# Strassen products for every other pair of feature blocks, plain products for the rest

## The chip, the cores and the metric

The kernel runs on one core of one Trainium2 chip. The metric is the device time of one execution in microseconds (us). Before the change three timed runs took 3019.33, 3019.34 and 3024.54 us (median 3019.34). Below, PE is TensorE's matmuls and PEld its weight loads, DVE is VectorE, ACT is ScalarE, POOL is GpSimd and SP is SyncE, which issues most DMAs.

## The reference

Two stages follow each other. The first transforms 8 sequences of 3008 tokens by 256 channels with a real FFT along the tokens, mixes the channels with a complex 256x256 matrix, adds a bias, shrinks the values and transforms back. The second is a two-layer network on the 24064 rows that result:

```python
X = np.fft.rfft(x, axis=1)
Yr = Xr @ w_r - Xi @ w_i + b_r ;  Yi = Xr @ w_i + Xi @ w_r + b_i
Yr, Yi = shrink(Yr, 0.01), shrink(Yi, 0.01)
y = np.fft.irfft(Yr + 1j * Yi, n=3008, axis=1)      # rows of 256
h = y @ w_in                                        # 256 -> 2048
g = np.maximum(h, 0.0) ** 2
out = g @ w_out                                     # 2048 -> 256
```

The change lies in the last line, `g @ w_out`.

## The kernel before

**Tiles and steps.** The 24064 rows are cut into 48 tiles (`tiles`, six for each of the 8 sequences) of 500 or 504 columns: the kernel holds everything transposed, features in the partitions, tokens along the columns. The 2048 features are 16 blocks of 128. A `Step(t, n)` takes tile t and the pair of feature blocks 2n and 2n+1, so a tile has 8 steps (n = 0 to 7) and the kernel 384. Each number is carried as a sum of two shorter ones, hi and lo, and every product is three matmuls: hi by hi, lo by hi, hi by lo. `win`, `wout` and the tiles `yt`, `mb`, `mt` are such couples.

**What a step does.** `block(j)` multiplies the tile by `w_in` for block j of the pair: 6 matmuls of 500 columns into a bank `psh` (there are two). ACT takes relu out of the bank (`mc<-psh`); for j = 0 DVE squares it (`mc<-psh,mc`), for j = 1 ACT squares it (`mc<-mc`). `mc` then holds four quarters: two feature blocks by two halves of the tokens. Those are the four entries of a 2x2 block matrix, and the 256 rows of `w_out` that belong to the pair, by its 256 output columns, are the other. `out(j)` multiplies the two by Strassen's scheme in Winograd's form: 7 products of 128x128 by 128x250 in place of 8. Three of them take quarters of `mc` as they are (`raw`), four take the sums T1 to T4 that POOL makes of them (`ms`, three instructions). The weights' sums S1 to S4 are made once, at the start. `split` makes hi and lo of the raw quarters (`mb`, an ACT cast and a DVE subtraction), `split_sums` of the sums (`mt`, likewise). `out(0)` is the 9 matmuls on `mb`, `out(1)` the 12 on `mt`, all of 250 columns; they add up over the tile's 8 steps in four banks (`pso0` to `pso3`).

**The tile's end.** The four banks then hold products that still have to be added to one another. `drain` copies the banks to `me` (DVE: banks 0 and 3, ACT: banks 1 and 2) and `finish` adds them on POOL, six instructions, and stores two tiles of output.

**What sets the order.** In the main loop at the end, half-step m does, for n = m // 2 and k = m % 2: `steps[n-2].out(k)`, `steps[n].block(k)`, and for k = 1 `steps[n-1].split_sums()` and `steps[n].split()`. The helper `then` chains these instructions on each engine in just this order, so each engine's queue takes them one after the other. The transforms (`Fwd`, `Pair`, `Back`; banks `psf`) of the sequences that come next are put between them by a scheduling pass: in the first seven of the eight sequences the queues hold transform work as well, in the last one nearly none. Ahead of the main loop a front part transforms the first sequence in full precision and prepares the weights from 64-bit numbers; `moe_part`, `wout_join` and `wout_sums` belong to it.

Of the kernel before, what the change touches and what calls it, by code (L numbers as in the profile page):

```python
# [10 lines left out]
F32R = mybir.dt.float32r  # L11
# [25 lines left out]
    "kv": 3, "psf": 6,  # L37
}
MAIN = {
    "xs": 1, "xe": 1, "kv": 1, "kp": 1, "kq": 1, "ksh": 1, "ksl": 1, "kxl": 1, "kb": 1, "kcm": 1, "me": 1,  # L40
}


# [6 lines left out]

A11, A12, A22, S1, S2, S3, S4 = range(7)
B11, B22, B21 = range(3)
T1, T3, T2, T4 = range(4)


# [1 line left out]
def fnet_moe(ctx: ExitStack, tc, x, w_r, w_i, b_r, b_i, w_in, w_out, bm, cm, dx, a32, c32, out):  # L59
# [14 lines left out]
    wout = [const.tile([128, NF // 2, 7, 128], F32R, name=f"wout{j}") for j in range(2)]  # L74


    front = ExitStack()
# [91 lines left out]
    def moe_part(q):  # L169
        if q < 8:  # L170
            f, c = divmod(q, 2)
            fs = slice(f * 512, (f + 1) * 512)
            return Double(
                win[0][:, c, fs], win[1][:, c, fs], w_in[c * 128:(c + 1) * 128, f * 1024:(f + 1) * 1024],
                lambda t: t.rearrange("p f t -> p (f t)"),
            )
        f = (q - 8) * 2
        return Double(
            None, None, w_out[f * 128:(f + 2) * 128, :].rearrange("(f p) d -> p f d", p=128),
            lambda t: t.rearrange("p (f d) t -> p f (d t)", f=2),  # L180
        )

# [6 lines left out]
    def wout_sums(n, pair):  # L189
        w = pair[0].wide  # L190
        a = w.rearrange("p n (f i d) -> p n f i d", f=2, i=2)
        a11, a21, a12, a22 = (a[:, :, f, i] for f in range(2) for i in range(2))
        st = T("ds", [128, 2, 4, 128], F32)
        s1, s2, s3, s4 = (st[:, :, j] for j in range(4))
        dve.tensor_add(out=s1, in0=a21, in1=a22)
        sub(dve, s2, s1, a11)
        sub(dve, s3, a21, a11)
        sub(dve, s4, a12, s2)
        hi, lo = (v[:, n:n + 2] for v in wout)
# [262 lines left out]
    def then(eng, op, *args, **kwargs):  # L462
        with tc.issue_after(last_of[eng].ins) if eng in last_of else nullcontext():
            last_of[eng] = op(*args, **kwargs)  # L464

    def then_halves(hi, lo, v):
        then(act, copy, act, hi, v)
        then(dve, sub, dve, lo, v, hi)

    class Step:  # L470
# [3 lines left out]
        def block(self, j):  # L474
# [14 lines left out]
            if j == 0:  # L489
# [4 lines left out]
            self.raw, self.sum = (  # L494
                [T(f"m{v}{k}", [128, n * HM], F32R)[:, :n * h].rearrange("p (j h) -> p j h", j=n) for k in range(2)]
                for v, n in (("b", 3), ("t", 4))
            )
# [9 lines left out]
        def split_sums(self):  # L507
            then_halves(self.sum[0], self.sum[1], self.s)

        def out(self, j):  # L510
            t, n, h = self.t, self.n, self.h
            if n == j == 0:
                acc[t] = [bank([128, 2, 256], f"pso{d}")[:, :, :h] for d in range(4)]
            o = acc[t]

            products = (
                ((S4, self.raw, B22, o[0], 0), (A12, self.raw, B21, o[0], 1), (A11, self.raw, B11, o[1], 0)),
                ((S2, self.sum, T2, o[1], 1), (S1, self.sum, T1, o[2], 0), (S3, self.sum, T3, o[2], 1),
                 (A22, self.sum, T4, o[3], 0)),
            )[j]  # L520
            for a, g, b, ps, i in products:
                for k, (w, v) in enumerate(((0, 0), (1, 0), (0, 1))):
                    then(
                        pe, pe.matmul, ps[:, i], wout[w][:, n, a], g[v][:, b], start=n == k == i == 0,
                        stop=n == NF // 2 - 1 and k == 2 and (i == 1 or a == A22),
                    )
            if n == NF // 2 - 1:
                self.drain(j)

        def drain(self, j):  # L530
            t, h = self.t, self.h
            o = acc[t]
            if j == 0:
                e = T("me", [128, 8 * HM], F32)[:, :8 * h].rearrange("p (j h) -> p j h", j=8)
                acc[t].append(e)
                copy(dve, e[:, 0:2], o[0])
                return
            e = o[4]
            copy(act, e[:, 6:8], o[1])
            copy(act, e[:, 4:6], o[2])  # L540
            copy(dve, e[:, 3], o[3][:, 0])


        def finish(self, k):
            t, h = self.t, self.h
            e = acc[t][4]
            c22, c21, p5, p7, p1, u2 = (e[:, j] for j in range(2, 8))
            if k == 6:
# [7 lines left out]
            add = (  # L556
                (u2, u2, p1), (c22, p5, p7), (e[:, 4:6], e[:, 4:6], u2.unsqueeze(1).broadcast_to([128, 2, h])),
                (e[:, 0:2], e[:, 0:2], e[:, 4:8:2]), (c22, c22, u2), (c21, c21, p7),
            )[k]
            pool.tensor_tensor(out=add[0], in0=add[1], in1=add[2], op=ALU.add)  # L560


    def pair_tasks(pairs, start, step):
# [34 lines left out]

    ring = [Fwd32(0, q, 2) for q in range((J + 1) // 2)]
    units = [Unit32(0, g) for g in range(G)]  # L600
    parts = [moe_part(q) for q in (0, 1, 8, 9, 2, 3, 10, 11, 4, 5, 12, 13, 6, 7, 14, 15)]

    for f in ring[:FRONT["big"]]:
        f.load()
# [7 lines left out]
    extra = []  # L612
    for n, p in enumerate(parts):
        k = n * 13 // 10
        if n % 4 == 2:
            extra += [(k + 3, lambda n=n: wout_join(parts[n:n + 2]))]
        extra += [(k - 1, p.load), (k + 3, lambda p=p, u=units[k]: p.bits(u)), (k + 3, p.join)]
        if n % 4 < 2:
            extra += [(k + 3, p.split)]
        elif n % 4 == 3:  # L620
            extra += [(k + 3, lambda n=n: wout_sums(n // 4 * 2, parts[n - 1:n + 1]))]
    extra.sort(key=lambda j: j[0])
    last = units[2]
    for r in range(-5, len(units) + 3):
# [28 lines left out]
    for m in range(2 * len(steps) + 11):  # L653
# [25 lines left out]
        if ends:  # L679
            ends.pop(0)()  # L680
        if k and n % (NF // 2) == 1 and n > 1:
            ends += [lambda u=steps[n - 2], j=j: u.finish(j) for j in range(7)]
        while jobs and jobs[0][0] < r + 1:
            jobs.pop(0)[1]()

# [85 lines left out]
```

## Time and profile before

| | |
|---|---|
| median of 3 runs | 3019.34 us |
| the profiled execution: its time, its span | 3021.53 us, 3019.6 us |
| PE busy | 2707.3 us (90%), 16856 matmuls |
| POOL, DVE, ACT busy | 2277.0 (75%), 1984.2 (66%), 1757.7 us (58%) |
| mean granted TensorE clock | 0.976 |
| DMA | 250.41 MB, 83 GB/s on the mean |
| first matmul of the main loop (`psh`) | 156 us from the start |

The span runs from the first to the last instruction, and the busy time of PE is the union of its matmuls' records, whose ends are modelled: a matmul's record is longer than the time until the next may start. So PE's time is read below from the starts of matmuls that follow each other, and from its waits.

### The profile page before, as it was taken

Reading aid. Unit: us, or ns where it says so; the run is one execution under the profiler, and the core shown is the slowest. Engines: PE = TensorE matmul, PEld = TensorE weight load, DVE = VectorE, ACT = ScalarE, POOL = GpSimd, SP = SyncE. Lnnn points to the kernel's source line nnn. Section 1 sums busy time; section 2 is a strip of 40 time slices with the busy share of each in tenths; the row PEclk is TensorE's granted clock in tenths of the full one; section 3 lists DMA queues with packets and bytes.
Section 4 is the critical chain, followed back from the end, with each engine's and each line's share of the span. In section 5 each row is a group of like instructions: output and inputs, shape, how many; then the busy total and the mean of one; then the engine's idle time right before and its main releaser. Section 6 shows DMA issues by size and latency. Waiting matters only on the chain.

```text
span 3019.6 us, 46324 instructions
## 1 busy us (share of the span) xinstructions
PE 2707.3 (90%) x16856; PEld 2392.2 (79%) x16856; DVE 1984.2 (66%) x2651; ACT 1757.7 (58%) x3178; POOL 2277.0 (75%) x2082
## 2 busy tenths in 40 slices
PE   5699988899999999999999998999999999988887
PEld 4588877788878888888878888888887888877776
DVE  5846676577657766577656777567765777755554
ACT  3465655565556655656556565566656666555554
POOL 3387768687788867878788777888778886777776
PEclk8899999899999999999999999999999999999999
DMA  8432233322242223322323222322224222210000
GB/s 242 156 104 89 65 94 90 99 79 86 66 115 73 84 79 89 100 77 77 91 85 94 75 84 80 99 80 79 84 64 123 73 75 74 74 40 23 30 8 14
DMA packets 191253, 250.41 MB, mean 83 GB/s; under 512 B 21755, under 2 KB 135667, under 8 KB 191027
## 3 DMA queue, kind: packets, MB, share of 16 engines
q1 hardware_dynamic: 178627, 224.85, 24.5%
q0 software_dynamic: 12400, 22.61, 3.4%
q8 instruction: 134, 2.20, 0.3%
q14 instruction: 92, 0.75, 0.1%
HBM read 146.85 MB, written 100.53 MB: 82 GB/s over the span
## 4 chain that ended last, share of the span: by engine, by line
PE 36%; DVE 19%; POOL 18%; ACT 14%; issue 6%; DMA 2%; SPq 0%; POOLq 0%; DVEq 0%; ACTq 0%
PE pso L464 15%; PE psh L464 15%; DVE mt L94 10%; POOL ms L94 7%; ACT mt L90 6%; ACT mc L464 5%; POOL me L560 5%; POOL xs L233 4%; PE psf L301 4%; DVE kv L322 3%; DVE mb L94 2%; DMA du<-s 1%; POOL yt L94 1%; PE psf L236 1%; DVE mc L464 1%
## 5 line engine op out<-in xcount | busy, mean ns | idle before, releaser
L464 PE MATMUL psh<-yt,win 128*128 128x500 f32 (+1 forms) x4608 | 1211.6, 396 | 1.4 <-DVE mc L464 1.2
L94 DVE TENSOR_TENSOR mt<-ms,mt 128x1000 fp32r<-128x1000 f32 (+1 forms) x384 | 579.1, 1508 | 711.1 <-ACT mt L90 710.3
L464 PEld LDWEIGHTS psh<-yt,win 128*128 128x128 f32 x4608 | 825.3, 191 | 125.1 <-DVE mc L464 2.0
L94 POOL TENSOR_TENSOR ms<-mc,ms 128x250 f32<-128x250 f32 (+1 forms) x768 | 875.7, 1140 | 46.5
L464 PE MATMUL pso<-mt,wout 128*128 128x250 f32 (+1 forms) x4608 | 711.6, 293 | 193.6 <-DVE mt L94 167.5
L464 ACT ACTIVATE mc<-psh 128x500 f32<-128x500 f32 (+1 forms) x768 | 451.9, 588 | 697.3 <-PE psh L464 694.7
L464 PEld LDWEIGHTS pso<-mt,wout 128*128 128x128 f32 x4608 | 607.3, 192 | 282.8 <-DVE mt L94 223.4
L94 POOL TENSOR_TENSOR ms<-mc 128x500 f32<-128x500 f32 (+1 forms) x384 | 503.8, 1312 | 330.4 <-ACT mc L464 318.1
L94 DVE TENSOR_TENSOR mb<-mc,mb 128x750 fp32r<-128x750 f32 (+1 forms) x384 | 540.6, 1408 | 3.2 <-ACT mb L90 2.5
L464 PE MATMUL pso<-mb,wout 128*128 128x250 f32 (+1 forms) x3456 | 501.6, 283 | 1.7 <-DVE mb L94 1.7
L464 PEld LDWEIGHTS pso<-mb,wout 128*128 128x128 f32 x3456 | 473.8, 190 | 34.1 <-DVE mb L94 1.9
L90 ACT CAST mt<-ms 128x1000 fp32r<-128x1000 f32 (+1 forms) x384 | 391.6, 1020 | 62.6 <-POOL ms L94 62.3
L90 ACT CAST mb<-mc 128x750 fp32r<-128x750 f32 (+1 forms) x384 | 314.4, 819 | 0.0
L560 POOL TENSOR_TENSOR me<-me 128x250 f32<-128x250 f32 (+3 forms) x288 | 295.3, 1048 | 15.3 <-ACT me L90 12.5
L464 DVE SCALAR_TENSOR_TENSOR mc<-psh,mc 128x500 f32<-128x500 f32 (+1 forms) x384 | 256.5, 668 | 12.7 <-ACT mc L464 11.1
L464 ACT ACTIVATE mc<-mc 128x500 f32<-128x500 f32 (+1 forms) x384 | 239.8, 625 | 9.2
L94 POOL TENSOR_TENSOR yt<-dy,yt 128x376 fp32r<-128x376 f32 (+3 forms) x168 | 149.9, 894 | 114.6 <-ACT yt L90 113.7
L233 POOL TENSOR_TENSOR xs<-xt 120x256 f32<-120x256 f32 x182 | 187.1, 1048 | 35.4 <-PE psf L236 34.5
L301 PE MATMUL psf<-wx,kxh 128*128 128x256 f32 x1008 | 203.6, 282 | 4.6 <-DVE kul L94 4.6
L90 ACT CAST yt<-dy 128x376 fp32r<-128x376 f32 (+3 forms) x168 | 71.8, 432 | 192.9 <-DVE dy L446 119.9
L322 DVE TENSOR_TENSOR kv<-psf,ke 64x256 f32<-64x256 f32 x336 | 141.2, 420 | 46.2 <-PE psf L301 41.9
L301 PEld LDWEIGHTS psf<-wx,kxh 128*128 128x128 f32 x1008 | 165.0, 189 | 8.0 <-DVE kul L94 6.0
(89 smaller groups left out, 2680.3 us busy)
## 6 DMA issues: line engine op xcount, KB each, us to landing
du<-s SPq DMA_DIRECT2D x128, 256.0 KB, 3.1
s<-kuh SPq DMA_DIRECT2D x192, 128.0 KB, 2.1
s<-kul SPq DMA_DIRECT2D x192, 128.0 KB, 2.1
s<-xe SPq DMA_DIRECT2D x92, 240.0 KB, 2.4
xt<-x_in SPq DMA_DIRECT2D x91, 240.0 KB, 3.1
kcm<-cm_in POOLq DMA_DIRECT2D x84, 256.0 KB, 3.5
ka<-s SPq DMA_DIRECT2D x84, 256.0 KB, 3.2
du<-s SPq DMA_DIRECT2D x256, 64.0 KB, 3.0
```

Of the source, the lines that this page charges most:

```text
L90: return act.copy(out=out, in_=in_)
L94: return eng.tensor_tensor(out=out, in0=a, in1=b, op=ALU.subtract)
L233: pool.tensor_tensor(out=u[:, t], in0=self.xt[:, 0, 0], in1=self.xt[:, 0, 1], op=(ALU.add, ALU.subtract)[t])
L236: nc.tensor.matmul(ps[:M1, t], am32[:, t], u[:, t], start=True, stop=True)
L301: self.last = nc.tensor.matmul(ps, l, wx[j][:, k, c, :], start=n == 0, stop=n == 5)
L322: dve.tensor_add(out=v[64 * r:64 * r + 64, g], in0=ps[gs], in1=self.e[gs, r])
L464: last_of[eng] = op(*args, **kwargs)
L560: pool.tensor_tensor(out=add[0], in0=add[1], in1=add[2], op=ALU.add)
```

## The change

Steps with even n keep Strassen's scheme. Steps with odd n multiply plainly: 4 weight blocks by the quarters, with both token halves in one matmul of 500 columns, 12 matmuls in place of 21. Their results are added straight to bank 0 and bank 3, where the output quarters of the two feature halves of the output build up; banks 1 and 2 get products of even steps alone. The product of A22 and T4 moves from the first half of bank 3 to the second.

Odd steps have no `ms` (POOL), no `mt` (ACT and DVE); their `mb` holds four quarters instead of three (1000 columns for 750). `mb` gets three buffers. Banks 1 and 2 are drained after step 6, banks 0 and 3 after step 7, and these copies and POOL's additions (now five) are chained by `then` too. The weights' sums are made for four pairs of blocks instead of eight (`wsum`), the other four are kept as they are (`wout`), and the order of the weights' parts in the front is another.

```diff
         def split(self):
-            then_halves(self.raw[0], self.raw[1], self.c[:, 1:])
+            n = 1 - self.n % 2
+            then_halves(self.raw[0][:, n:], self.raw[1][:, n:], self.c[:, n:])
 
         def split_sums(self):
+            if self.n % 2:
+                return
             then_halves(self.sum[0], self.sum[1], self.s)
...
+            end = NF // 2 - 1
+            if n % 2:
+                for d in range(2):
+                    dsl = slice(d * 128, d * 128 + 128)
+                    for k, (w, v) in enumerate(((0, 0), (1, 0), (0, 1))):
+
+                        begins = d and n == 1 and j == k == 0
+                        for cut in (slice(0, 1), slice(1, 2)) if begins else (slice(0, 2),):
+                            then(
+                                pe, pe.matmul, o[3 * d][:, cut], wout[w][:, n - 1 + j, dsl],
+                                self.raw[v][:, 2 * j:2 * j + 2][:, cut],
+                                start=False, stop=n == end and j == 1 and k == 2,
+                            )
+            else:
+
+                products = (
+                    ((S4, self.raw, B22, o[0], 0), (A12, self.raw, B21, o[0], 1), (A11, self.raw, B11, o[1], 0)),
+                    ((S2, self.sum, T2, o[1], 1), (S1, self.sum, T1, o[2], 0), (S3, self.sum, T3, o[2], 1),
+                     (A22, self.sum, T4, o[3], 1)),
+                )[j]
...
+            if n == end - 1 and j == 1:
                 e = T("me", [128, 8 * HM], F32)[:, :8 * h].rearrange("p (j h) -> p j h", j=8)
                 acc[t].append(e)
-                copy(dve, e[:, 0:2], o[0])
-                return
-            e = o[4]
-            copy(act, e[:, 6:8], o[1])
-            copy(act, e[:, 4:6], o[2])
-            copy(dve, e[:, 3], o[3][:, 0])
+                then(act, copy, act, e[:, 6:8], o[1])
+                then(act, copy, act, e[:, 4:6], o[2])
+            if n == end and j == 1:
+                e = o[4]
+                then(dve, copy, dve, e[:, 0:2], o[0])
+                then(act, copy, act, e[:, 2:4], o[3])
```

Three places of the queues show it. The first is PE in the fifth sequence: the second part of a step's `out`, up to the next `psh` (names ending in 81, 83 and 85 are hi parts of weights, 82, 84 and 86 lo parts). Before, its last seven rows (products S3 and A22, then the next block's first matmul):

```order
L464 MATMUL pso_18025<-mt_18263,wout_83 128x252
L464 MATMUL pso_18025<-mt_18263,wout_84 128x252
L464 MATMUL pso_18025<-mt_18264,wout_83 128x252
L464 MATMUL pso_18026<-mt_18263,wout_83 128x252
L464 MATMUL pso_18026<-mt_18263,wout_84 128x252
L464 MATMUL pso_18026<-mt_18264,wout_83 128x252
L464 MATMUL psh<-yt_17198,win_81 128x504
```

And the second part of an odd step now, whole:

```order
L467 MATMUL pso_16308<-mb_16613,wout_83 128x2x252
L467 MATMUL pso_16308<-mb_16613,wout_84 128x2x252
L467 MATMUL pso_16308<-mb_16614,wout_83 128x2x252
L467 MATMUL pso_16311<-mb_16613,wout_83 128x2x252
L467 MATMUL pso_16311<-mb_16613,wout_84 128x2x252
L467 MATMUL pso_16311<-mb_16614,wout_83 128x2x252
L467 MATMUL psh<-yt_15568,win_81 128x504
```

An odd step's second part reads `mb` alone and writes banks 0 and 3 with both halves at once.

The second place is DVE at a tile's end in the last sequence, before:

```order
L464 SCALAR_TENSOR_TENSOR mc<-psh,mc 128x500
L91 COPY me<-pso_31022 128x500
L94 TENSOR_TENSOR mt_31356<-ms,mt_31355 128x1000
L94 TENSOR_TENSOR mb_31406<-mc,mb_31405 128x750
L464 SCALAR_TENSOR_TENSOR mc<-psh,mc 128x500
L91 COPY me<-pso_31025 128x250
L94 TENSOR_TENSOR mt_31408<-ms,mt_31407 128x1000
L94 TENSOR_TENSOR mb_31463<-mc,mb_31462 128x750
```

And now:

```order
L96 TENSOR_TENSOR mb_26983<-mc,mb_26982 128x750
L467 SCALAR_TENSOR_TENSOR mc<-psh,mc 128x500
L93 COPY me<-pso_26620 128x504
L96 TENSOR_TENSOR mt_26985<-ms,mt_26984 128x1000
L96 TENSOR_TENSOR mb_27041<-mc,mb_27040 128x1000
L467 SCALAR_TENSOR_TENSOR mc<-psh,mc 128x500
L96 TENSOR_TENSOR mb_27096<-mc,mb_27095 128x750
```

One `mt` in two steps is left, the `mb` of odd steps is wider, and the copy of bank 0 stands ahead of the `mt` that follows.

The third place is PE in the fifth sequence (step 204 of 384, an even one): from the last matmul of a block to the third matmul on `mt`, the first that reads its lo part. Before:

```order
L464 MATMUL psh<-yt_17199,win_81 128x504
L333 MATMUL psf<-ksh,kcm 128x256 x2
L333 MATMUL psf<-ksl,kcm 128x256
L464 MATMUL pso_18024<-mt_18263,wout_83 128x252
L464 MATMUL pso_18024<-mt_18263,wout_84 128x252
L464 MATMUL pso_18024<-mt_18264,wout_83 128x252
```

And now:

```order
L467 MATMUL psh<-yt_15569,win_81 128x504
L467 MATMUL pso_16309<-mt_16532,wsum_85 128x252
L467 MATMUL pso_16309<-mt_16532,wsum_86 128x252
L443 MATMUL psf<-dx_sb,du 128x2x94
L446 MATMUL psf<-dx_sb,du 128x2x94
L447 MATMUL psf<-dx_sb,du 128x188
L467 MATMUL pso_16309<-mt_16533,wsum_85 128x252
```

The transforms' matmuls stand at other places between the steps, since the scheduling pass has laid them out anew.

More of the change, by code (lines that the diff above doesn't have):

```diff
@@ L73, in fnet_moe @@
     win = [const.tile([128, 2, FF], F32R, name=f"win{j}") for j in range(2)]
-    wout = [const.tile([128, NF // 2, 7, 128], F32R, name=f"wout{j}") for j in range(2)]
+    wout = [const.tile([128, NF // 2, D], F32R, name=f"wout{j}") for j in range(2)]
+    wsum = [const.tile([128, NF // 4, 7, 128], F32R, name=f"wsum{j}") for j in range(2)]
     front = ExitStack()
@@ L514, in out @@
             o = acc[t]
[L516 to L533, printed above, removed]
+            end = NF // 2 - 1
[16 more added lines that the diff above has]
+                )[j]
+                for a, g, b, ps, i in products:
+                    for k, (w, v) in enumerate(((0, 0), (1, 0), (0, 1))):
+                        then(
+                            pe, pe.matmul, ps[:, i], wsum[w][:, n // 2, a], g[v][:, b],
+                            start=n == k == 0 and (i == 0 or a == A22),
+                            stop=n == end - 1 and k == 2 and a in (S2, S3),
+                        )
@@ L546, in finish @@
             e = acc[t][4]
-            c22, c21, p5, p7, p1, u2 = (e[:, j] for j in range(2, 8))
-            if k == 6:
+            if k == 5:
                 b, c0, _ = tiles[t]
@@ L600, in fnet_moe @@
     units = [Unit32(0, g) for g in range(G)]
-    parts = [moe_part(q) for q in (0, 1, 8, 9, 2, 3, 10, 11, 4, 5, 12, 13, 6, 7, 14, 15)]
+    order = (0, 1, 8, 10, 2, 3, 9, 11, 4, 5, 12, 14, 6, 7, 13, 15)
+    parts = [moe_part(q) for q in order]
     for f in ring[:FRONT["big"]]:
@@ L681, in fnet_moe @@
         if k and n % (NF // 2) == 1 and n > 1:
-            ends += [lambda u=steps[n - 2], j=j: u.finish(j) for j in range(7)]
+            ends += [lambda u=steps[n - 2], j=j: u.finish(j) for j in range(6)]
         while jobs and jobs[0][0] < r + 1:
```

41 lines of the change are left out of this document (24 added, 17 removed).

## The prediction, made before the changed kernel ran

> **What bounds the kernel now.** I read the page's busy times and its chain first.
>
> ```profile
> PE 2707.3 (90%) x16856; PEld 2392.2 (79%) x16856; DVE 1984.2 (66%) x2651; ACT 1757.7 (58%) x3178; POOL 2277.0 (75%) x2082
> PE 36%; DVE 19%; POOL 18%; ACT 14%; issue 6%; DMA 2%; SPq 0%; POOLq 0%; DVEq 0%; ACTq 0%
> ```
>
> PE is busiest, yet only 36% of the chain is its work: it is handed from PE to ACT, POOL and DVE and back. Where PE then stands still is told by the groups (columns: line, engine, operation, tiles, shapes, count; busy us, mean ns of one; idle us of the engine before them and what ended it):
>
> ```profile
> L464 PE MATMUL psh<-yt,win 128*128 128x500 f32 (+1 forms) x4608 | 1211.6, 396 | 1.4 <-DVE mc L464 1.2 <-POOL yt L94 0.2
> L464 PE MATMUL pso<-mt,wout 128*128 128x250 f32 (+1 forms) x4608 | 711.6, 293 | 193.6 <-DVE mt L94 167.5 <-ACT mt L90 22.5
> L464 PE MATMUL pso<-mb,wout 128*128 128x250 f32 (+1 forms) x3456 | 501.6, 283 | 1.7 <-DVE mb L94 1.7
> L94 DVE TENSOR_TENSOR mt<-ms,mt 128x1000 fp32r<-128x1000 f32 (+1 forms) x384 | 579.1, 1508 | 711.1 <-ACT mt L90 710.3
> L94 DVE TENSOR_TENSOR mb<-mc,mb 128x750 fp32r<-128x750 f32 (+1 forms) x384 | 540.6, 1408 | 3.2 <-ACT mb L90 2.5
> L94 POOL TENSOR_TENSOR ms<-mc,ms 128x250 f32<-128x250 f32 (+1 forms) x768 | 875.7, 1140 | 46.5
> L94 POOL TENSOR_TENSOR ms<-mc 128x500 f32<-128x500 f32 (+1 forms) x384 | 503.8, 1312 | 330.4 <-ACT mc L464 318.1 <-DVE me L91 6.8 <-DVE mc L464 2.5
> L90 ACT CAST mt<-ms 128x1000 fp32r<-128x1000 f32 (+1 forms) x384 | 391.6, 1020 | 62.6 <-POOL ms L94 62.3
> L90 ACT CAST mb<-mc 128x750 fp32r<-128x750 f32 (+1 forms) x384 | 314.4, 819 | 0.0
> ```
>
> Of all groups of the main loop only the matmuls on `mt`, the split Strassen sums, wait for long. Those on `mb` wait 1.7 us. Who waits for `mt` (us, times; the first row gives min/median/max ns of DVE's `mt`):
>
> ```profile
> L94 DVE TENSOR_TENSOR mt<-ms,mt x384: 1189/1454/2424, 169.0 to 3008.9; 128x1000 fp32r<-128x1000 f32 x128, 128x1008 fp32r<-128x1008 f32 x64
>   PEld pso L464: 268.1, 344
>   PE pso L464: 190.0, 240
> ```
>
> How the wait comes about is clearest in the last sequence, where hardly any transform is left. The chain of waits there, over one step:
>
> ```profile
> 2827.74 1.36 DVE mt L94
> 2829.10 0.04 issue
> 2829.14 1.42 PE pso L464 x10
> 2830.57 1.36 PE psh L464 x6
> 2831.93 0.02 issue
> 2831.96 0.60 ACT mc L464
> 2832.55 0.02 issue
> 2832.58 0.02 ACT mc L464
> 2832.60 0.51 issue
> 2833.11 1.03 ACT mt L90
> 2834.13 0.02 issue
> 2834.15 1.36 DVE mt L94
> ```
>
> This is a loop of 6.41 us: the last 10 matmuls on `mt`, the second block of a later step, its relu and square on ACT, and only then, since `then` queues it there, the cast of the next `mt`, DVE's subtraction, and PE again. After that block PE has 9 matmuls on `mb`, one `psh` block and two matmuls on `mt` hi to do; the third on `mt` reads lo and waits. In the first seven sequences transform matmuls fill part of the hole. By window (columns: us, PE, PEld, DVE, ACT, POOL busy, clock, DMA share, GB/s), a middle sequence and the last:
>
> ```profile
> 1263.00:1621.00 358.00, 332.79 (x2117) 296.78 (x2116) 241.25 (x320) 216.82 (x391) 282.94 (x263) 0.99 0.29 84
> 2683.00:3013.00 330.00, 280.80 (x1683) 239.56 (x1681) 181.21 (x185) 182.07 (x298) 241.41 (x203) 0.99 0.07 21
> ```
>
> The last has a fifth fewer matmuls, yet is 28 us shorter only. POOL is at 79% in the middle, PE at 93%. So: a PE kernel with a hole in every step, made by the route of the sums.
>
> **The change part by part.** The sum is made against the median, 3019.3 us. The profiled execution took 3021.5 us (span 3019.6), 2.2 us above it; that is below all that follows.
>
> *Plain products, 192 steps.* Two rows of PE give the paces:
>
> ```profile
> 2830.41 1.51 PE L464 MATMUL psh<-yt,win 128*128 128x500 f32 x6
> 2831.76 1.22 PE L464 MATMUL pso<-mb,wout 128*128 128x250 f32 x9
> 2798.77 0.25 PE L440 MATMUL psf<-dx_sb,du 128*128 128x188 f32 x1
> 2798.86 0.27 PE L443 MATMUL psf<-dx_sb,du 128*128 128x188 f32 x1
> ```
>
> With the mean record of one (396 and 283 ns) taken off, 500 columns follow each other every (1.51-0.396)/5 = 0.223 us, 250 every (1.22-0.283)/8 = 0.117. The chain has 1.36/6 = 0.227 for the former. Twelve at 0.225 are 2.70 us, the 21 they replace 2.46: **+0.24 us a step, +47 us** (0.223 to 0.227: +42 to +51). The trace shows no 500-column matmul written in two halves; the nearest rows are the last two above, 188 columns in two halves, 0.09 us from start to start, 0.48 ns a column against 0.47 for 250. I take no price for the halves.
>
> The Trainium skill speaks against the pace. "TensorE: Matmul & The Clock Gate", section Back-to-back issue gap, gives for streams of weight loads and matmuls a sustained 131 ns at 512 columns, where these rows have 223 at 500. By it twelve plain products would be an estimated 1.57 us, and the term -171 us instead of +47. The trace decides: the `psh` rows are such a stream.
>
> *The hole of odd steps.* They have no `mt`, and their `mb` is ready long before. The loss in all steps lies between two rows: PE idle 190.0 us plus, in 240 waits, a record's tail in which PE could have gone on (0.293-0.117): 232 us; and PEld idle 268.1 plus 344 times (0.192-0.117): 294. (0.192 us is a weight load's record, from the next row.) I take the upper, since a weight load's wait is seen where it happens.
>
> ```profile
> L464 PEld LDWEIGHTS pso<-mt,wout 128*128 128x128 f32 x4608 | 607.3, 192 | 282.8 <-DVE mt L94 223.4 <-ACT mt L90 44.7
> ```
>
> Half of it is **-147 us** (-116 by the other).
>
> *The hole of even steps.* The place in the queues is the same: relu, square, `mt` cast, `mt` subtraction after an odd step's second block. Two things narrow it. POOL's `ms` of the next step, which now runs beside DVE's `mt`, is gone, as odd steps have none; DVE's `mt` takes 1.508 us on the mean and 1.189 at best. If it comes down to 1.24, each hole that ends with DVE (PE counts some half of the steps, PEld more) gets 0.27 shorter: 100 to 160 of 192 of them, **-35 us**. And the new order holds more transform work in the hole: counted over the middle sequences and priced at 0.105 to 0.12 us a matmul, 1.36 us on the mean, against 0.93 (even) and 1.34 (odd steps) before: 0.23 us more, but only where a hole is not closed already: **-15**. Bounds: nothing narrows, 0; all closes, -147.
>
> *POOL, ACT, DVE.* 192 times 1.312+2x1.140 = 3.59 us leave POOL (690 us), 1.02 leave ACT, 1.5 leave DVE; `mb` grows by a third, some 0.2 us on ACT and 0.4 on DVE. None of this is on the path beyond the hole counted above. In the last sequence, after an odd step's second block, its `mb` lo is there some 5.3 us later (relu and square 1.3, `mt` 1.0 and 1.2, `mb` 1.5 and queueing), and PE, behind the even step's `out` with its hole and two blocks, asks for it after 6.3 us. If that cover is gone it costs up to 0.4 us a step, +77; I take 0. The relu behind ACT's wider cast is late by 0.2 us, and its bank is not asked for again until a plain product and a block later.
>
> *Tile ends and front.* Bank 0 is copied on DVE while PE does a `psh` block of 1.36 us; it stands ahead of `mt`. POOL adds the same number of columns in five instructions. In the front fewer sums of weights are made. All at 0, within 5 us.
>
> *What surfaces.* The other waits of the main loop's PE are short in the groups; a denser PE meets the transforms' waits sooner, POOL's relief makes them shorter. 0, within 20 us.
>
> Sum: 3019.3 + 47 - 147 - 35 - 15 = **2869 us**. Cross-check in the last sequence: two steps are 12.82 us by the loop; now 6.41 - 0.12 for the even one's loop, and the odd one adds four pieces of 1.36: 11.73. Over 24 pairs -26 us, and more where POOL's additions now end the chain.
>
> **The rivals.**
>
> *A: only half goes.* DVE's `mt` stays at 1.5 us beside POOL's other work, the extra cover falls where no hole is, and the odd steps' wider `mb` shows a little. For it: most of a step's POOL time next to `mt` is transforms in the middle sequences. Against: `ms` is 1380 of POOL's 2277 us. 3019 + 47 - 147 = 2919, with some `mb` waits 2930.
>
> *B: the holes close.* With half the work off POOL and less on ACT and DVE, `mt` is there in time: 3019 + 47 - 294 = 2772. For it: only 344 of 384 steps waited at all. Against: the loop's ACT and DVE parts are in series behind PE's own block and no relief shortens the 2.3 us of ACT.
>
> *C: slower, since plain products don't stream.* If a 500-column matmul into two halves of a bank took its whole record, 0.396 us, an odd step would be 4.75 us, +2.29, +440 us: 2822 + 440 = 3262. It decides against the change from (2.46 + 197/192)/12 = 0.29 us a matmul. Against it: the `psh` and the two-half rows.
>
> *D: the gain is spent at tile ends.* Banks 0 and 3 now come free only after a tile's last product. If the first product of the next tile waited until DVE had done `mt` and `mb` too, 3 us at 47 ends, 141 us would go: 3010. Against it: the copy stands ahead of `mt` in DVE's queue.
>
> *E: the page's pace.* 12 wide products overlapping to 131 ns: 3019 - 171 - 197 = 2651.
>
> **How the numbers follow.** The forecast, 2869, has 0.61, with 2835 to 2905 as its own range (loss 232 or 294, the rest within 20); A 0.18; B 0.13; C 0.04; D 0.03; E 0.01. The range is 2815 to 2940: it takes in A, and leaves out most of B, C, D and E, together 0.2. A measurement of this kernel can tell 0.2% from no change, and by that 0.93 are faster, 0.03 the same (D's neighbourhood), 0.04 slower.
>
> **What will show it.** In the changed profile PE's matmuls on `mt` should be released by DVE in at most 192 waits, with PE's idle time there at 60 us or less, and DVE's `mt` near 1.25 us. The wide products, `pso` from `mb` and `wout`, should have a mean record near 396 ns and follow each other every 0.225 us: 0.29 would be C. POOL's busy time should be near 1590 us and PE's share over 93%. `mb` among the releasers of `pso` with over 20 us would be A, PE waiting for a DVE `me` copy at every tile's end D. PE idle at `mt` of over 90 us would prove the step on the even holes wrong.

## The result, and the profile after

The changed kernel takes 2848.5 us (median of four runs, 2846.34 to 2851.95) against 3019.34: a ratio of 0.9432 with a 95% interval of 0.9416 to 0.9449, 171 us less. The profiled execution took 2851.95 us (span 2850.1).

The page of the kernel after, busy times and the chain by engine:

```profile
PE 2689.5 (94%) x15176; PEld 2343.3 (82%) x15176; DVE 1661.8 (58%) x2401; ACT 1674.7 (59%) x3032; POOL 1458.8 (51%) x1458
PE 77%; DVE 6%; ACT 6%; issue 3%; DMA 2%; POOL 2%; SPq 0%; POOLq 0%; ACTq 0%; DVEq 0%
```

PE's share of the chain went from 36 to 77%, DVE's from 19 to 6, POOL's from 18 to 2. The groups after (columns as before: busy us, mean ns of one, idle us ahead and what ended it):

```profile
L467 PE MATMUL psh<-yt,win 128*128 128x500 f32 (+1 forms) x4608 | 1210.0, 396 | 8.7 <-ACT yt L92 8.3 <-POOL yt L96 0.4
L467 PE MATMUL pso<-mb,wout 128*128 128x500 f32 (+3 forms) x2352 | 611.3, 387 | 0.0
L467 PE MATMUL pso<-mt,wsum 128*128 128x250 f32 (+1 forms) x2304 | 338.5, 290 | 42.1 <-DVE mt L96 38.0 <-ACT mt L92 2.3
L467 PE MATMUL pso<-mb,wsum 128*128 128x250 f32 (+1 forms) x1728 | 250.5, 284 | 0.0
L96 DVE TENSOR_TENSOR mb<-mc,mb 128x1000 fp32r<-128x1000 f32 (+3 forms) x384 | 533.4, 1389 | 392.8 <-ACT mb L92 389.8
L96 DVE TENSOR_TENSOR mt<-ms,mt 128x1000 fp32r<-128x1000 f32 (+1 forms) x192 | 252.2, 1313 | 354.6 <-ACT mt L92 353.7
L96 POOL TENSOR_TENSOR ms<-mc,ms 128x250 f32<-128x250 f32 (+1 forms) x384 | 356.4, 928 | 25.5
```

The plain products (`pso` from `mb` and `wout`) and the raw Strassen products wait for nothing at all; the matmuls on `mt` wait 42.1 us where they waited 193.6. Who waits for `mt` after the change:

```profile
L96 DVE TENSOR_TENSOR mt<-ms,mt x192: 1190/1202/2251, 164.8 to 2835.4; 128x1000 fp32r<-128x1000 f32 x128, 128x1008 fp32r<-128x1008 f32 x64
  PEld pso L467: 62.2, 94
  PE pso L467: 40.2, 54
```

PE waits 54 times (before: 240), and DVE's `mt` has its median at 1.202 us, close to its minimum, where it was 1.454. The chain of waits in the last sequence, two steps of it:

```profile
2653.96 1.21 DVE mt L96
2655.17 0.04 issue
2655.21 1.43 PE pso L467 x10
2656.64 1.35 PE psh L467 x6
2657.99 1.34 PE pso L467 x7
2659.34 1.36 PE psh L467 x6
2660.69 1.36 PE pso L467 x6
2662.06 1.37 PE psh L467 x6
2663.43 0.02 issue
2663.45 0.60 ACT mc L467
...
2664.60 1.02 ACT mt L92
2665.62 0.02 issue
2665.64 1.42 DVE mt L96
```

The loop through ACT and DVE is still there, once in two steps. Between two `mt` lie 11.68 us (2653.96 to 2665.64). Four pieces of 1.34 to 1.36 us in it wait for nothing; the loop itself, with one `psh` block, is the other 6.27 us, 0.14 less than the 6.41 before, as this `mt` takes DVE 1.21 us for 1.36. One of the four pieces, on PE's timeline:

```profile
2660.53 1.53 PE L467 MATMUL pso<-mb,wout 128*128 128x500 f32 x6
```

With a mean record taken off, (1.53 - 0.387)/5 = 0.229 us from one wide product to the next.

To compare all kernels I split their main loops from the starts of PE's matmuls. "Work" is each matmul's number times the pace at which its kind follows itself undisturbed (0.228 us for 500 columns, 0.1165 for 250, 0.118 for 256, 0.104 for 188 and 0.105 for 128 in the transforms, 0.215 for 256 in their widest kind; in proportion for 504 and 252). "Rest" is what the main loop takes beyond it, and "at mt" is the part of the rest that lies ahead of matmuls on `mt`. "Half clock" is the time in the main loop during which the trace records a granted clock of 0.5; at most half of it is lost by the clock and stands in the rest (after the change the matmuls' doubled spacings in these stretches add up to 36 of the 106 us). "5th" and "last" are the lengths of two of the eight sequences. These are from the profiled executions, in us; each ratio is to runs of the kernel before that were made beside that kernel's own.

| kernel | median | ratio to before (95%) | work | rest | at mt | half clock | 5th | last |
|---|---|---|---|---|---|---|---|---|
| before | 3019.34 | 1 | 2459.5 | 396.0 | 306 | 96 | 355.8 | 328.7 |
| after | 2848.5 | 0.9432 (0.9416 to 0.9449) | 2515.0 | 172.4 | 80 | 106 | 341.4 | 298.1 |
| plain_all | 2833.24 | 0.9388 (0.9368 to 0.9407) | 2570.8 | 108.0 | 0 | 86 | 339.3 | 273.7 |
| early_before | 2995.12 | 0.9914 (0.9884 to 0.9943) | 2459.6 | 370.2 | 269 | 155 | 366.7 | 307.0 |
| early_after | 2782.65 | 0.9222 (0.9208 to 0.9235) | 2515.0 | 104.9 | 7 | 41 | 330.7 | 286.6 |
| narrow | 2808.84 | 0.9308 (0.9290 to 0.9327) | 2526.8 | 122.6 | 96 | 34 | 331.7 | 301.2 |
| odd21 | 2745.34 | 0.9108 (0.9090 to 0.9125) | 2459.5 | 122.0 | 100 | 33 | 323.9 | 288.3 |
| keepms | 2890.25 | 0.9586 (0.9570 to 0.9602) | 2515.0 | 210.1 | 114 | 106 | 344.5 | 301.8 |
| shift | 2868.63 | 0.9516 (0.9501 to 0.9532) | 2515.0 | 192.8 | 95 | 109 | 343.0 | 302.2 |
| early_swap | 2754.71 | 0.9137 (0.9123 to 0.9151) | 2515.0 | 75.8 | 4 | 43 | 331.1 | 273.3 |
| early_keepms | 2780.04 | 0.9215 (0.9199 to 0.9231) | 2515.0 | 103.3 | 24 | 48 | 333.8 | 278.0 |
| keepall | 2996.79 | 0.9942 (0.9920 to 0.9964) | 2515.0 | 312.0 | 128 | 136 | 363.1 | 303.8 |
| early_narrow | 2766.20 | 0.9169 (0.9154 to 0.9184) | 2526.9 | 75.1 | 7 | 17 | 330.2 | 286.1 |
| swap_narrow | 2713.40 | 0.8987 (0.8974 to 0.8999) | 2526.8 | 21.8 | 6 | 15 | 323.3 | 274.5 |

From before to after: work +55.5, rest -223.6, of which -226 ahead of `mt`, and the front to the first `psh` -3.2 (156.1 to 152.8). Together -171; some 2 us more stand behind PE's last matmul, so the profiled spans differ by 169.5.

### The profile page after: what moved, and what is told of

Read it like the earlier page. It is cut to its first block, busy times and chain, and to the rows that moved or that the text cites. A ratio compares the mean times of both kernels' runs of the same rounds, so it can differ in the third digit from the quotient of the medians.

```text
span 2850.1 us, 41765 instructions
## 1 busy us (share of the span) xinstructions
PE 2689.5 (94%) x15176; PEld 2343.3 (82%) x15176; DVE 1661.8 (58%) x2401; ACT 1674.7 (59%) x3032; POOL 1458.8 (51%) x1458
## 4 chain that ended last, share of the span: by engine, by line
PE 77%; DVE 6%; ACT 6%; issue 3%; DMA 2%; POOL 2%; SPq 0%; POOLq 0%; ACTq 0%; DVEq 0%
PE psh L467 31%; PE pso L467 31%; PE psf L304 6%; DVE mt L96 3%; PE psf L239 3%; PE psf L283 2%; ACT mc L467 2%; ACT mt L92 2%; PE psf L336 2%; DMA s<-xe 1%; POOL xs L236 1%; DVE kv L325 1%; PE psf L447 1%; PE psf L446 1%; PE psf L443 1%
## 5 line engine op out<-in xcount | busy, mean ns | idle before, releaser
L96 DVE TENSOR_TENSOR mb<-mc,mb 128x1000 fp32r<-128x1000 f32 (+3 forms) x384 | 533.4, 1389 | 392.8 <-ACT mb L92 389.8
L467 PE MATMUL pso<-mb,wout 128*128 128x500 f32 (+3 forms) x2352 | 611.3, 387 | 0.0
L96 POOL TENSOR_TENSOR ms<-mc 128x500 f32<-128x500 f32 (+1 forms) x192 | 233.3, 1215 | 545.4 <-ACT mc L467 536.9
L96 DVE TENSOR_TENSOR mt<-ms,mt 128x1000 fp32r<-128x1000 f32 (+1 forms) x192 | 252.2, 1313 | 354.6 <-ACT mt L92 353.7
L467 PE MATMUL pso<-mt,wsum 128*128 128x250 f32 (+1 forms) x2304 | 338.5, 290 | 42.1 <-DVE mt L96 38.0
L96 POOL TENSOR_TENSOR ms<-mc,ms 128x250 f32<-128x250 f32 (+1 forms) x384 | 356.4, 928 | 25.5
L467 PEld LDWEIGHTS pso<-mt,wsum 128*128 128x128 f32 x2304 | 304.2, 194 | 72.7 <-DVE mt L96 54.4
L92 ACT CAST mb<-mc 128x1000 fp32r<-128x1000 f32 (+3 forms) x384 | 355.6, 926 | 5.0
L467 POOL TENSOR_TENSOR me<-me 128x500 f32<-128x500 f32 (+3 forms) x240 | 275.5, 1156 | 37.1 <-ACT me L92 31.4
L467 PE MATMUL pso<-mb,wsum 128*128 128x250 f32 (+1 forms) x1728 | 250.5, 284 | 0.0
```

Source lines behind the costliest of these rows:

```text
L92: return act.copy(out=out, in_=in_)
L96: return eng.tensor_tensor(out=out, in0=a, in1=b, op=ALU.subtract)
```

## The experiments

H is the theory that the gain comes from the waits of PE at `mt` that are no longer there. P says that it comes from the work that POOL, ACT and DVE no longer have. S, in the second group, says that it matters where the scheduling pass lays the transforms.

### Holes, or width: four kernels

**plain_all**: every step is plain, 12 matmuls of 500 columns. No sums, no `mt`, two banks, nothing to add at a tile's end.

```diff
-            if n % 2:
-                for d in range(2):
+            for d in range(2):
...
-                                pe, pe.matmul, o[3 * d][:, cut], wout[w][:, n - 1 + j, dsl],
+                        pe, pe.matmul, o[d], wout[w][:, 2 * n + j, dsl], self.raw[v][:, 2 * j:2 * j + 2],
...
-                then(act, copy, act, e[:, 6:8], o[1])
-                then(act, copy, act, e[:, 4:6], o[2])
```

> All eight steps of a tile multiply plainly (12 wide matmuls); no sums, no mt, two banks instead of four, no additions at a tile's end. Theory H (PE lost its time in the hole before the mt matmuls; a plain step costs PE 0.24 to 0.28 us more): the rest of the holes, 62 us idle of PEld plus 94 x 0.077 us = 69 us, goes, 192 more plain steps cost +47 to +54: 2825 to 2835 us. Rival P (the gain came from the relief of POOL, ACT and DVE): the relief is had once more in full, so another 100 to 170 us go: 2680 to 2750. A slower time than 2860 would say that the plain products cost more than their pace.

2833.2 us: H. The page of plain_all:

```profile
PE 2719.0 (96%) x13400; PEld 2293.3 (81%) x13400; DVE 1340.1 (47%) x2199; ACT 1525.1 (54%) x2742; POOL 552.2 (19%) x642
```

POOL falls from 1459 to 552 us, and the gain over the change is 15 us: 80 fewer ahead of `mt`, 56 more of work, and other waits. So as the changed kernel stands, what the four Strassen steps of a tile save PE in matmuls is spent on their holes. Relief of POOL beyond what the change gives is worth nothing visible here.

**early_before** and **early_after**: in the kernel before and in the changed one, the cast and the subtraction of `mt` are queued half a step earlier, behind the first block of the next step in place of the second.

```diff
-        if k and 0 < n <= len(steps):
+        if not k and 0 < n <= len(steps):
             steps[n - 1].split_sums()
```

> The kernel before with one edit: split_sums of step n-1 is queued in the half-step k = 0 of step n, half a step earlier, so ACT's cast and DVE's subtraction of mt no longer stand behind the square of the next step. Theory H (the hole is made by the place in the queues): most of the loss of 232 to 294 us goes: 2750 to 2830 us, as far as POOL has the sums ready by then. Rival P (mt is late since POOL, at 75 to 80%, is late with the sums): ACT now waits for POOL and holds up the relu behind it, no gain: 3000 to 3080.

> The changed kernel with the same edit (only even steps have sums). Theory H: the rest of the holes, 69 us, closes for the most part, since POOL is idle half the time: 2780 to 2805 us. Rival P: what is left of the holes is not a matter of the queue's place: 2840 to 2860.

In the changed kernel the holes close: 7 us ahead of `mt` where 80 were, 2782.65 us, as H has it. Before the change the same edit brings 24 us, which neither theory gave. The waits of early_before (us, times, longest):

```profile
ACT mt L90 <- POOL ms L94: 559.3, 292, 6.4
...
PEld pso L464 <- DVE mt L94: 156.5, 175, 4.4
...
PEld pso L464 <- ACT mt L90: 75.0, 72, 2.4
```

ACT now comes to the cast before POOL has made the sums: 559 us of waiting where the kernel before had 62. So P has a part too. POOL is still late for the earlier place in early_after, though by less:

```profile
ACT mt L92 <- POOL ms L96: 159.0, 139, 2.6
```

There PE hardly notices: its matmuls wait 0.2 us for `mt`. Whether it is POOL's relief that makes the earlier place worth 66 us is asked below, by early_keepms.

In early_after a new wait appears, which has no row after the change:

```profile
PE pso L467 <- DVE me L93: 39.1, 27, 2.4
```

DVE's copy of bank 0 at a tile's end now stands behind the earlier `mt` in DVE's queue, and the next tile's first product waits for it.

**narrow**: the plain products as 24 matmuls of 250 columns.

```diff
-                        for cut in (slice(0, 1), slice(1, 2)) if begins else (slice(0, 2),):
+                        for cut in (slice(0, 1), slice(1, 2)):
...
```

> The changed kernel with each plain product of 500 columns cut into two matmuls of 250: 24 in an odd step instead of 12. By the paces of the trace (0.117 for 250, 0.225 to 0.227 for 500 columns) 24 x 0.117 - 12 x 0.226 = +0.10 us a step, +18 us: 2862 to 2872. If the wide ones did not stream at their pace (theory C of the prediction) the narrow ones would be no slower: 2848 or less.

2808.8 us, 40 us faster where 18 slower was expected; 2848 or less was named as the sign of theory C. C is out all the same: in the changed kernel 1704 wide products follow another one directly, and the median from start to start is 0.227 us, as for `psh`. PE's own part came out nearly as foreseen: work +12 and the last sequence +3.1 us (298.1 to 301.2). What I had not counted is that the scheduling pass lays the transforms elsewhere when the matmuls are others: most sequences with transforms are 5 to 10 us shorter, and less time runs at half clock, 34 us where 106 were. The mean clock of after, then of narrow:

```profile
core 0: 2850.1 us, clock 0.974
```

```profile
core 0: 2810.6 us, clock 0.986
```

0.012 of 2850 us is 34 us, and half of 106 - 34 is 36. That is the most that the clock can account for; counted at the matmuls whose spacing doubles it is 24 (36 less 12). What is left of the 40 is other waits.

### The relief, the places of the transforms, and the copies

**odd21**: odd steps issue 21 matmuls of 250 columns, on raw quarters.

```diff
-                for d in range(2):
-                    dsl = slice(d * 128, d * 128 + 128)
+                for d, i, a, b in ((0, 0, S4, 1), (0, 1, A12, 2), (3, 0, A11, 3)) if j == 0 else (
+                    (3, 1, S2, 0), (0, 0, S1, 1), (0, 1, S3, 2), (3, 0, A22, 3)
+                ):
                     for k, (w, v) in enumerate(((0, 0), (1, 0), (0, 1))):
...
+                        then(
+                            pe, pe.matmul, o[d][:, i], wsum[w][:, n // 2, a], self.raw[v][:, b],
...
```

> The changed kernel, but an odd step issues Strassen's 21 matmuls of 250 columns in place of the 12 wide ones, on the raw quarters that it has (so its sums are left out and the output isn't the reference's); nothing else of its work changes. Theory H: this gives back the price of the plain products, 0.24 to 0.28 us a step: -47 to -54 us, 2795 to 2802. In the last sequence, where no transforms are laid between the steps, 24 odd steps give -6 us of 298. If the plain form costs nothing, both stay; a second theory, S (the transforms' new places between the steps are worth some 40 us by themselves, as the narrow run suggested), puts up to 40 us either way on the whole time but not on the last sequence.

2745.3 us, below what either theory gave. The work falls by 55.5 as it must, the last sequence by 9.8 us (some 0.4 us for each of its 24 odd steps). The other 48 us are half clock again (106 to 33, at most 37 us) and other waits of the middle sequences. So where transforms hardly interfere the plain products cost 0.4 us a step by this run, 0.29 by the paces (12 of 0.228 against 21 of 0.1165), and the total cannot be used to price them: a change of PE's order moves the transforms too.

**shift**: the same work, with the transforms' tasks asked for at other times.

```diff
-                first, step = 1.0, 6.1
+                first, step = 2.0, 6.1
...
-                jobs += fwd_tasks(b + 2, 75.0, 1.4) + [(95.0, pairs[b + 2][0].load)]
+                jobs += fwd_tasks(b + 2, 73.0, 1.5) + [(95.0, pairs[b + 2][0].load)]
```

> The changed kernel with the transforms' tasks laid elsewhere between the steps: a sequence's pairs begin one half-step later, the next one's first transforms two half-steps earlier, 1.5 instead of 1.4 apart. All work is the same. Theory S (places where transforms crowd stall PE and halve its clock, twice per sequence in the changed kernel; 106 us of the main loop at half clock against 34 in the narrow run): the time moves by 10 to 40 us, and half of the change in half-clock time is part of it. Without S: 2840 to 2857.

2868.6 us, 20 us more, with 15 of it ahead of `mt`. S's size holds: the places alone are worth some tens of us. Its reason for half of them, the clock, doesn't: 106 and 109 us at half clock.

**keepms**: odd steps keep POOL's three sums; nothing reads them.

```diff
-            if self.n % 2:
-                return
             self.sum = [
```

> The changed kernel, but odd steps still make their three sums on POOL, and nobody reads them. Theory H (odd steps gain since PE waits for no mt there; POOL's relief only narrows the even steps' holes): DVE's mt goes back from 1.31 to 1.5 us and the even holes from 69 to 100 or 110 us: 2875 to 2900. Rival P (POOL's relief is the gain): most of the 170 us is lost: 2950 to 3010.

2890.3 us, 42 more: H's range. Who waits for `mt` in keepms:

```profile
L96 DVE TENSOR_TENSOR mt<-ms,mt x192: 1199/1460/2681, 163.2 to 2870.0; 128x1000 fp32r<-128x1000 f32 x128, 128x1008 fp32r<-128x1008 f32 x64
  PEld pso L467: 93.8, 137
```

With POOL's sums back, DVE's `mt` has its median at 1.460 us again, for 1.202, and PE's weight loads wait 93.8 us for 62.2. That is POOL's work beside DVE lengthening DVE's instruction, as the prediction's step on even steps says. The 42 us should hold little of places: of the 3796 transform matmuls in the main loop 598 stand in another half-step than in the changed kernel, where shift moved 2570.

**early_swap**: early_after, with the two copies at a tile's end exchanged between DVE and ACT.

```diff
-                then(dve, copy, dve, e[:, 0:2], o[0])
-                then(act, copy, act, e[:, 2:4], o[3])
+                then(act, copy, act, e[:, 0:2], o[0])
+                then(dve, copy, dve, e[:, 2:4], o[3])
```

> The run with the sums split half a step earlier, and with one edit more: at a tile's end ACT copies bank 0 and DVE bank 3, instead of the other way round. In that run PE waited 39 us in 27 waits for DVE's copy of bank 0, which stood behind mt (the prediction's rival D at a new place). Theory D2: ACT's copy stands ahead of that, so 25 to 40 us go: 2745 to 2760. If the copy only waits on ACT instead, the time stays: 2775 to 2785.

2754.7 us, in D2's range, and DVE's copy is gone from PE's waits. A smaller wait for ACT's copy stands in its place:

```profile
PE pso L467 <- ACT me L92: 8.4, 9, 1.9
```

So most of the wait at the tile's end in early_after came from DVE's queue.

### How much of the gain hangs on the relief

**early_keepms**: early_swap with POOL's unread sums in odd steps, by the same edit as in keepms.

> The run with the early split and the swapped copies (2754.7 us), with POOL's three sums of odd steps kept and unread. Theory R (the early place only closes the holes where POOL has the sums ready by then; in the kernel before it had not, and ACT waited 559 us for POOL instead): ACT's cast of mt waits for POOL clearly longer than the 200 us of that run, and 40 to 110 us are lost: 2795 to 2865. If POOL has nothing to do with it: 2750 to 2765.

2780.0 us, 25 more, between the two ranges. ACT's wait for POOL's sums grows from 201.5 us in early_swap to

```profile
ACT mt L92 <- POOL ms L96: 287.6, 160, 4.5
```

and 20 us come back ahead of `mt`. The direction is R's, the size below its range, which began at 40 more. Read the other way, with POOL's sums kept the earlier place and the swapped copies bring 110 us (keepms 2890.3 to 2780.0), without them 94 (2848.5 to 2754.7). These totals hold the transforms' places too, but the last sequence, which has none between its steps, says the same: 24 us with the sums (301.8 to 278.0) and 25 without (298.1 to 273.3). So the earlier place owes little of its worth to POOL's relief. In the kernel before it brings 22 us in the last sequence as well (328.7 to 307.0) and next to nothing in the seven others; why is not shown.

**keepall**: the changed kernel, whose odd steps make the sums, their cast and their subtraction as before; PE reads none of them.

```diff
-            if self.n % 2:
-                return
             self.sum = [
...
         def split_sums(self):
-            if self.n % 2:
-                return
             then_halves(self.sum[0], self.sum[1], self.s)
```

> The changed kernel (2848.5 us) with the odd steps' whole second route kept and unread: POOL's sums, ACT's cast and DVE's subtraction of mt. PE has no more to wait for than in the changed kernel. Theory H (PE gains because odd steps do not wait): all engines carry more than in the kernel before, yet most of the gain stays: 2880 to 2940. Rival P (the gain is the relief of the three engines): at least the time of before minus nothing: 2990 to 3080.

2996.8 us: P's range, and 148 of the 171 us are gone again, although PE's odd steps still have no `mt`. The waits ahead of `mt` stay short (128 us for 306); what takes the gain is 55 us more of PE's work and 94 us more of other rest than before the change. H is right for the last sequence alone: 303.8 us there, so 25 of the 30.6 us stay. In the fifth sequence nothing stays (363.1; before 355.8, after 341.4). PE's waits in keepall:

```profile
PEld pso L467 <- DVE mt L96: 97.6, 111, 2.0
...
PEld psf L239 <- POOL xs L236: 39.2, 49, 3.4
...
PE pso L467 <- DVE me L93: 18.2, 17, 1.9
```

And the first two after the change, where the third has no row:

```profile
PEld pso L467 <- DVE mt L96: 54.4, 75, 2.0
...
PEld psf L239 <- POOL xs L236: 23.2, 22, 1.8
```

Against the changed kernel the time comes back in many places (the profiled executions are 140 us apart): 48 us ahead of `mt`, 92 in the rest elsewhere (transforms that wait for POOL, DVE or ACT, tile ends), of which at most 15 are half clock. From keepms to keepall the edit adds one cast of 1.0 us on ACT and one subtraction of about 1.5 us on DVE in each odd step, and the time grows by 107 us. They stand in the same queues as the transforms' own casts and sums. But the scheduling pass has also laid the transforms elsewhere: 2146 of the 3796 transform matmuls stand in another half-step than in the changed kernel. A part of the 148 us can therefore be the places, which S names: they were worth 20 us in shift, and the rest fell by 50 with other orders in narrow and odd21. The two parts were not separated. In the last sequence, where no transforms are laid between the steps, keepall costs 5.7 us.

### The width of the products, once more

**early_narrow** and **swap_narrow**: early_after and early_swap with 24 narrow plain products for 12 wide ones, by the same edit as in narrow.

> The run with the early split (2782.7 us), with the plain products in 24 matmuls of 250 columns instead of 12 of 500. Both runs with wide and narrow products now have little half-clock time (41 us in the wide one), so the order of the transforms should disturb less: by the paces +0.10 us a step, +18 us: 2792 to 2812. If narrow ones are no slower: 2783 or less.

> The fastest run so far (early split, swapped copies, 2754.7 us) with the plain products in 24 matmuls of 250 columns: the third pair of wide and narrow. Theory W (the narrow form costs its pace, 0.07 us a step in the runs' traces, +13 us, and what the two earlier pairs gained came from the transforms' places and the clock): 2755 to 2775 unless half-clock time falls well below the 43 us of the wide run. Theory N (narrow products are better for PE by themselves): again 15 to 40 us less, 2715 to 2740, and less in the last sequence too, where the wide run takes 273 us.

early_narrow takes 2766.2 us, 16 less than early_after and not the 10 to 30 more that the paces gave, again with less half clock (41 to 17) and the same last sequence (286.6 and 286.1). swap_narrow is the fastest kernel of all, 2713.4 us, a ratio of 0.8987 (0.8974 to 0.8999). Its page and the groups on `mt` and the plain products:

```profile
PE 2632.1 (97%) x17432; PEld 2410.9 (89%) x17432; DVE 1657.1 (61%) x2401; ACT 1692.6 (62%) x3032; POOL 1502.1 (55%) x1458
```

```profile
L467 PE MATMUL pso<-mb,wout 128*128 128x250 f32 (+1 forms) x4608 | 635.8, 281 | 0.4 <-DVE mb L96 0.3
L467 PE MATMUL pso<-mt,wsum 128*128 128x250 f32 (+1 forms) x2304 | 321.0, 281 | 1.2 <-DVE mt L96 1.2
```

22 us of rest are left in its main loop. The time is 1.6 us below N's range, and W left room for it, as half-clock time fell to 15 us. N's second mark isn't met: the last sequence is 1.2 us longer than with wide products (274.5 for 273.3), so the narrow form is no better for PE itself where no transforms stand between. The 41 us come from the middle sequences, at most 14 of them from the clock. Why the narrow form does better among transforms, three times in three, by the places that the scheduling pass finds or otherwise, stays open.

## Why the prediction was right, and which steps were not

2869 was forecast, 2848.5 measured; its own range, 2835 to 2905, holds it.

**What bounds the kernel** was right. The hole at `mt` was what kept PE from its work: with the odd steps' holes gone PE is 77% of the chain, and with the queue place mended as well (early_after) nine tenths of what was left there is gone (80 to 7 us).

**Plain products, +47** was a little small. By the paces it is +55.5 us: 0.228 us a wide product (0.225 was taken) and 0.1165 a narrow one, 0.29 us a step for 0.24. The row of 0.229 stands above. In the last sequence odd21 puts the price higher, at 0.4. Rival C needed 0.29 us a product and rival E 0.131. The Trainium skill's 131 ns at 512 columns ("TensorE: Matmul & The Clock Gate", section Back-to-back issue gap) isn't seen with these 500-column matmuls either: 229 ns in that row.

**The hole of odd steps, -147**: by the starts of the matmuls on `mt`, odd steps lost 157 of the 306 us before and even ones 148, so half was the right share, and all of the odd ones' went.

**The holes of even steps, -35 and -15**: mis-sized. PE's weight loads still wait 62.2 us in 94 waits, with the prediction's tail of 0.075 us each 69 us, where 97 (294 - 147 - 35 - 15) was forecast. This is the larger part of the miss. By the starts the 148 us of the even steps become 128 in keepall, 114 in keepms and 80 after the change: -20 with the new order and cover alone (-15 forecast), -34 for POOL's sums that no longer lengthen DVE's `mt` (-35 forecast), and -14 for the cast and subtraction of odd steps, of which the sum had nothing. The -20 and the -14 are no surer than places allow: shift alone moved this column by 15.

**"None of this is on the path beyond the hole counted above"**, on the work taken from POOL, ACT and DVE, is the step that failed. keepms costs 42 us and keepall 148, the latter with an unknown share of places: in the seven sequences with transforms, the three engines' queues hold work that PE asks for, and keepall's rows show PE waiting for it when the relief is withheld, though the odd holes are gone. The sum came out since it counted the odd holes as gone and everything that could take their place as nothing, and with the relief that was so: the rest other than at `mt` is 90 us before and 92 after. The number was right, the reason half of it.

**"What surfaces: 0, within 20"** was met (+2) but the bound is too narrow for its reason. shift moved 20 us with the same work, narrow 40 and more. Where the scheduling pass would lay the transforms wasn't known, and 0 was partly luck.

**The rivals.** A is out: `mb` is no releaser of `pso`, and DVE's `mt` is down to 1.313 us on the mean. B's 2772 is not the change's, but nearly that of early_after (2783), which closes the holes by other means. D is not in the changed kernel and appears in early_after and keepall, with 39 and 18 us in place of 141. E's 0.131 us is excluded by the 0.227. **What was to show it:** 54 waits (at most 192), 42.1 us (at most 60), 1.313 us for `mt` (1.25), 387 ns for a wide record (396), PE 94% (over 93): as written or close to it. POOL's 1459 us are below the 1590 forecast, as its instructions are shorter too, with less beside them (928 ns for 1140).

By terms: 2869, +8 for the plain products, -29 at `mt`, +2 for other waits, -3 for the front, some +2 behind PE's last matmul: 2849, for 2848.5 measured.

## What to carry to other kernels

When a change removes a wait on the busiest engine and also takes work off the engines that feed it, run it once with that work kept and unread: here 23 of 171 us were left then, and without that run the whole would have been put down to the wait. Look in that run at the order of the busiest engine too, since it may have changed with the edit. A cheaper algorithm for the busiest engine (7 products for 8) pays only if its operands are there in time, so look at the place of their making in the feeding engines' queues before counting matmuls: half a step earlier was worth 66 us, and one copy exchanged between two queues 28. And where a scheduler lays work around the change, run the same work at other places: a total that moves by 20 to 40 us with the places cannot price a smaller step, and a stretch without that work can.

## What the runs showed of the hardware

The granted clock falls to half in the middle of the main loop, where PE's longest pause is under 2 us. In the third to the sixth sequence of the changed kernel it does so twice in each. Around one of these falls, three neighbouring windows (columns: us, PE, PEld, DVE, ACT, POOL busy, clock, DMA share, GB/s) and PE's timeline:

```profile
1400.00:1414.60 14.60, 12.68 (x81) 11.30 (x79) 8.63 (x15) 7.33 (x14) 3.91 (x5) 1.00 0.19 55
1414.70:1421.40 6.70, 5.55 (x20) 4.95 (x20) 4.32 (x8) 4.02 (x9) 3.03 (x4) 0.50 0.59 174
1421.60:1436.00 14.40, 14.40 (x87) 12.85 (x86) 7.91 (x13) 7.29 (x12) 6.15 (x8) 1.00 0.30 85
```

```profile
1411.42 0.28 PE L304 MATMUL psf<-wx,kxh 128*128 128x256 f32 x1
1413.62 1.13 PE L283 MATMUL psf<-kb,ka 128*128 128x128 f32 x8 [1.92 <-issue]
1415.90 2.87 PE L467 MATMUL psh<-yt,win 128*128 128x500 f32 x6 [1.15 <-ACT yt L92]
...
1424.05 1.52 PE L467 MATMUL psh<-yt,win 128*128 128x500 f32 x6
```

Six `psh` matmuls take 2.87 us at half clock, and 1.52 a little later. The fall is recorded at 1414.7 us, behind the pause of 1.92 us and a burst of eight matmuls; the pause of 1.15 us already lies in the half-clock stretch. Four more falls of this kind (recorded at 1073.4, 1752.6, 2094.0 and 2435.3 us) also have one pause of 1.92 us as the only one above 0.3 us in the 7 us before them. The falls between them (1189.4, 1527.4, 1868.7 and 2210.0 us) follow three pauses or more of 0.63 to 0.95 us, 2.4 us or more in all. And one pause of 1.93 us, at 733.7 us, is followed by no fall. All such stretches in the main loop add up to 106 us after the change and to 15 in the fastest kernel. The Trainium skill warns of pauses above some 3 us ("TensorE: Matmul & The Clock Gate", section Why this matters for your kernels); here the clock falls behind shorter ones, of 1.92 us or below. What decides between a fall and none wasn't tested.

POOL's work beside DVE lengthens DVE's `mt` of 128x1000: a median of 1.202 us after the change, 1.454 before and 1.460 in keepms, at the same minimum of 1.19 to 1.20. Within the changed kernel's own trace, the 111 `mt` that have POOL idle for over nine tenths of their time take 1.20 us on the mean, the 72 that have it busy for over half of it 1.47.
